# Issuing the second chunk of the first projection's weights from ScalarE instead of SyncE

## Chip, cores, metric

The kernel runs on one core of a Trainium2 chip. The metric is the device time of one execution in microseconds, the median over several runs.

## The reference

Two independent attention blocks, A and B, on their own inputs; the outputs are joined along the last axis. Per block, in bf16:

```python
# x: 16 x 32 x 1024, caches: 16 x 4 x 512 x 128, wq: 1024 x 4096, wo: 4096 x 1024
q = (x @ wq).reshape(B, Sq, Hq, Dh).transpose(0, 2, 1, 3)      # 32 heads of 128
k = repeat(k_cache, 8, axis=1); v = repeat(v_cache, 8, axis=1)
p = softmax(einsum("bhqd,bhkd->bhqk", q, k) * Dh ** -0.5)
out = einsum("bhqk,bhkd->bhqd", p, v).transpose(0, 2, 1, 3).reshape(B, Sq, Hq * Dh) @ wo
```

## The kernel before

All products of both blocks form one stream on PE (TensorE). Nothing can be multiplied before the first rows of A's `x` and `wq` have landed, so the first eight heads are projected chunk by chunk (a chunk is 128 of the 1024 input rows) while the loads come in. `TT` is 4 (tiles of 128 tokens), `NF` is 6 heads, `HC` is 4 chunks.

```python
load_x(0, TT // 2, TT, nc.scalar)        # x0b, 128 KB, on ACT
nc.scalar.preload_act_table_set("natural_log_exp_and_others")
load_x(0, 0, TT // 2)                    # x0a, 128 KB, on SP like all below
load_w0(0, 1, 0, NF // 2)                # w0a, 96 KB
load_w0(0, 1, NF // 2, NF)               # w0b, 96 KB
load_w0(1, 2, 0, NF)                     # w1, 192 KB
load_x(2, 0, TT)                         # x2, 256 KB
load_w0(2, 3, 0, NF)                     # w2, 192 KB
load_w0(3, 4, 0, NF)                     # w3, 192 KB
# ... on SP: the rest of w0, transposed x, wq, k, v

warm_up(22)                              # 22 products of constants, 128 columns
for k, ts in enumerate(((0, TT // 2), (TT // 2, TT))):
    transpose_x(0, *ts, nc.vector.tensor_copy)          # needs x0a, then x0b
    transpose_x(1, *ts, nc.scalar.copy, spare[k])
for ts in ((0, TT // 2), (TT // 2, TT)):
    first_heads(range(0, NF // 2), (0,), *ts)           # 6 products, need w0a
first_heads(range(NF // 2, NF), (0,))                   # 3 products, need w0b
first_heads(range(0, NF - 2), (1,))                     # 4 products, need w1
transpose_x(2, 0, TT, nc.vector.tensor_copy)            # need x2
transpose_x(3, 0, TT, nc.scalar.copy)
first_heads(range(NF - 2, NF), (1,))                    # 2 products, need w1
first_heads(range(NF), (2, 3))                          # need w2, w3
# ... everything else follows on PE in program order
```

Of the kernel before, what the change touches and what calls it, by code (L numbers as in the profile page):

```python
# [181 lines left out]
def kernel(  # L182
# [14 lines left out]
    nc = tc.nc  # L197
# [20 lines left out]
    def fast_path(ok_i):  # L218
        with ExitStack() as fctx:
# [235 lines left out]
            NF = REP - 2  # L455
# [8 lines left out]
            def load_x(d0, t0, t1, eng=nc.sync):  # L464
                eng.dma_start(
                    out=x_sb[:, t0:t1, d0 * P:(d0 + 2) * P],
                    in_=x_v[:, t0:t1, d0 * P:(d0 + 2) * P],
                )
# [4 lines left out]
                    in_=A_x.flatten_outer_dims()[:, d0 * P:(d0 + 2) * P],  # L473
                )

            def load_w0(d0, d1, h0, h1):
                nc.sync.dma_start(
                    out=w0[d0 // HC][:, d0 % HC:(d1 - 1) % HC + 1, h0 * DH:h1 * DH],
                    in_=wq_v[:, d0:d1, h0 * DH:h1 * DH],
                )  # L480

            load_x(0, TT // 2, TT, nc.scalar)
            nc.scalar.preload_act_table_set("natural_log_exp_and_others")
            load_x(0, 0, TT // 2)
            load_w0(0, 1, 0, NF // 2)
            load_w0(0, 1, NF // 2, NF)
            load_w0(1, 2, 0, NF)
            load_x(2, 0, TT)
            load_w0(2, 3, 0, NF)
            load_w0(3, 4, 0, NF)  # L490
# [184 lines left out]
    ok_i = flag.tile([1, 1], I32, name="ok_i")  # L675
    total = 2 * 2 * NG * QW
    ok = fast_path(ok_i)
    with tc.If(ok < total, preferred_fallthrough_block=True, label="general"):
        general_path(tc, problems, out_flat)
# [30 lines left out]
```

## Time and profile before

| kernel before | value |
|---|---|
| time, median of 3 runs | 343.63 us (343.56 to 343.73) |
| profiled execution | 343.01 us, span 341.2 us |
| PE busy | 98% of the span |
| first transpose, first product with weights | 3.28 us, 4.17 us |
| PE's step from half to full clock, by the distance of its starts | between 5.0 and 5.2 us |

A line of the timeline gives start, duration, engine, source line, operation, operands and count, then the idle time before and what ended it. PE is the array, PEld its weight loads, which run ahead of it: a wait of PEld is a wait of PE only if PE runs out of products. In the DMA view q1 is SP's queue and q10 is ACT's.

### The profile page before, as it was taken

What the parts mean: (1) busy time and instruction counts of PE and PEld (TensorE: products, weight loads), DVE (VectorE), ACT (ScalarE), POOL (GpSimd) and SP (SyncE); (2) the same over time, 40 slices, a digit from 0 to 9 for tenths busy, and PEclk for the clock granted to TensorE, in tenths of its full rate; (3) what the DMA queues carried; (4) which work ended last, traced back from release to release, by engine and by line L of the source; (5) the groups of instructions that cost most, each with busy time, mean ns of one, the idle gap of its engine ahead of it and who ended that gap; (6) DMA issues with size and microseconds to landing.
All of it is one profiled execution on the core that took longest, in us unless ns stands there. A gap on an engine that the chain in (4) does not pass through costs nothing.

```text
span 341.2 us, 5454 instructions
## 1 busy us (share of the span) xinstructions
PE 335.2 (98%) x2082; PEld 213.6 (63%) x2121; DVE 265.5 (78%) x336; ACT 185.9 (54%) x209; POOL 46.7 (14%) x206
## 2 busy tenths in 40 slices
PE   8999999999999999999999999999999999999996
PEld 6455666666666666666666666666666666666555
DVE  1046988888988898888888988879888888889540
ACT  3058666666667667666645545555555555555110
POOL 0001110011111111110012221222122101111100
PEclk9999999999999999999999999999999999999999
DMA  7999999999996987899999955998449997430001
GB/s 211 287 190 273 285 249 202 233 242 268 291 248 154 232 242 219 210 314 299 308 306 258 250 125 144 334 268 242 118 103 296 356 187 176 104 97 16 18 18 33
DMA packets 128094, 71.70 MB, mean 210 GB/s; under 512 B 75840, under 2 KB 127296, under 8 KB 128064
## 3 DMA queue, kind: packets, MB, share of 16 engines
q1 hardware_dynamic: 127264, 70.07, 84.1%
q0 software_dynamic: 384, 1.05, 0.9%
q8 instruction: 17, 0.28, 0.3%
q10 hardware_dynamic: 416, 0.20, 0.2%
q14 instruction: 13, 0.11, 0.1%
HBM read 50.86 MB, written 2.10 MB: 155 GB/s over the span
## 4 chain that ended last, share of the span: by engine, by line
PE 98%; issue 1%; ACT 0%; ACTq 0%
PE f_ps L320 32%; PE q_ps L301 28%; PE ob L425 17%; PE s_ps L357 16%; PE q_ps L534 4%; PE q_ps L516 1%; PE xT_ps L524 0%; ACT o_sb L329 0%; ACTq L329 0%
## 5 line engine op out<-in xcount | busy, mean ns | idle before, releaser
L365 ACT ACTIVATE p_sb<-s_ps,shift 128x1024 bf16<-128x1024 f32 x128 | 142.7, 1115 | 97.5 <-PE s_ps L357 88.1
L376 DVE TRANSPOSE_TENSOR_REDUCE parts<-p_sb 128x32 f32<-128x1024 bf16 x128 | 158.7, 1240 | 21.0 <-ACT p_sb L365 19.3
L320 PE MATMUL f_ps<-wo_sb,oT 128*128 128x512 bf16 (+1 forms) x525 | 128.2, 366 | 0.6
L301 PE MATMUL q_ps<-xT,wq_sb 128*128 128x512 bf16 x430 | 113.2, 379 | 0.5
L425 PE MATMUL ob<-p_sb,v_sb 128*128 128x256 bf16 x512 | 76.8, 273 | 0.8
L357 PE MATMUL s_ps<-qT,kT 128*128 128x256 bf16 x512 | 76.8, 273 | 0.0
L320 PEld LDWEIGHTS <-oT 128*128 128x128 bf16 x544 | 53.2, 98 | 35.3
L357 PEld LDWEIGHTS <-kT 128*128 128x128 bf16 x512 | 56.9, 113 | 28.3
L301 PEld LDWEIGHTS <-wq_sb 128*128 128x128 bf16 x448 | 43.8, 98 | 32.2
L425 PEld LDWEIGHTS <-v_sb 128*128 128x128 bf16 x512 | 50.1, 98 | 20.0
L447 DVE TENSOR_TENSOR oT<-r,ob 128x512 bf16<-128x512 f32 x64 | 43.9, 686 | 19.9 <-PE ob L425 19.4
L411 DVE STREAM_TRANSPOSE r<-rall 128x512 f32<-128x512 f32 x64 | 44.2, 691 | 1.1
L309 ACT CAST qT<-q_ps 128x512 bf16<-128x512 f32 x56 | 32.7, 583 | 16.5 <-PE q_ps L301 16.5
L394 POOL COPY half<-cs 64x32 f32<-64x32 f32 x32 | 6.5, 204 | 231.8 <-DVE cs L384 231.8
L329 ACT CAST o_sb<-f_ps 128x512 bf16<-128x512 f32 (+1 forms) x17 | 9.5, 559 | 23.6 <-PE f_ps L320 23.6
L534 PE MATMUL q_ps<-xT,w_sb 128*128 128x512 bf16 (+1 forms) x65 | 14.4, 379 | 0.1
L384 DVE TENSOR_REDUCE cs<-parts 128x32 f32<-128x128 f32 x32 | 12.1, 377 | 1.1
L406 DVE RECIPROCAL rall<-sums 128x32 f32<-128x32 f32 x32 | 10.2, 319 | 3.3 <-POOL sums L403 3.3
L534 PEld LDWEIGHTS <-w_sb 128*128 128x128 bf16 x67 | 6.8, 102 | 7.0 <-DMA w_sb<-in_A_wq_dram 0.2
L560 DVE CAST qT<-q_ps 128x512 bf16<-128x512 f32 x4 | 2.5, 684 | 10.2 <-PE q_ps L534 10.2
L331 POOL DMA_DIRECT2D out_dram<-o_sb x8 | 4.6, 574 | 29.3 <-ACT o_sb L329 29.3
L395 POOL TENSOR_TENSOR half<-half,cs 64x32 f32<-64x32 f32 x32 | 7.8, 243 | 2.6
(25 smaller groups left out, 44.7 us busy)
## 6 DMA issues: line engine op xcount, KB each, us to landing
v_sb<-in_A_v_cache_dram SPq DMA_DIRECT2D x16, 512.0 KB, 5.7
wq_sb<-in_B_wq_dram SPq DMA_DIRECT2D x8, 1024.0 KB, 5.7
wo_sb<-in_A_wo_dram SPq DMA_DIRECT2D x8, 1024.0 KB, 7.4
v_sb<-in_B_v_cache_dram SPq DMA_DIRECT2D x16, 512.0 KB, 4.7
wo_sb<-in_B_wo_dram SPq DMA_DIRECT2D x8, 1024.0 KB, 8.1
wq_sb<-in_A_wq_dram SPq DMA_DIRECT2D x5, 1024.0 KB, 5.8
wq_sb<-in_A_wq_dram SPq DMA_DIRECT2D x2, 512.0 KB, 6.7
kT<-in_A_k_cache_dram SPq DMA_TRANSPOSE x64, 4.4
```

Of the source, the lines that this page charges most:

```text
L301: nc.tensor.matmul(ps[:], lhsT=w[:, dc, (h % 4) * DH:(h % 4 + 1) * DH], rhs=xT[pr][:, dc, :], start=(dc == 0), stop=(dc == DC - 1),)
L309: nc.scalar.copy(out=qT[pr, g][:, :, hl, :], in_=ps[:].rearrange("p (b s) -> p b s", s=SQ),)
L320: nc.tensor.matmul(ps[:, 0:width], lhsT=oT[pr, tt][:, h, :], rhs=wo_tiles[pr, nh, h // REP][:, h % REP, off:off + width], start=(h == 0), ...
L357: nc.tensor.matmul(s_ps[:, c, :], lhsT=kT[:, i % GRP, c, :], rhs=qT[pr, g][:, b, :, :].rearrange("p h s -> p (h s)"), start=True, stop=True,)
L365: nc.scalar.activation(out=p_sb[:], in_=s_ps[:], func=ACTF.Exp, bias=shift[:], scale=SCALE)
L376: nc.vector.tensor_reduce(out=parts[k][:, q, :, :].rearrange("p c h -> p (c h)"), in_=st[i]["p"][:].rearrange("p c (h s) -> p (c h) s", s=SQ),
L384: nc.vector.tensor_reduce(out=cs[:], in_=parts.pop(k)[:].rearrange("p q c h -> p q h c"), axis=AX.X, op=ALU.add,)
L406: nc.vector.reciprocal(out=rall[:, k, :], in_=quad.pop(k)[:])
L411: nc.vector.transpose(out=r[:].rearrange("p n s -> p (n s)"), in_=rall[:, k, o * 2 * REP:(o + 1) * 2 * REP] .unsqueeze(2).to_broadcast([P, ...
L425: nc.tensor.matmul(ob[j][:, q, :], lhsT=v_sb[:, i % GRP, c, :], rhs=st[i]["p"][:, c, :], start=(c == 0), stop=(c == KC - 1),)
L447: nc.vector.tensor_tensor(out=out, in0=rcp.pop(j)[:].rearrange("p (q h) s -> p q h s", h=REP), in1=ob.pop(j)[:].rearrange("p q (h s) -> p ...
L534: nc.tensor.matmul(first_q[h][:, ts], lhsT=w0[dc // HC][:, dc % HC, h * DH:(h + 1) * DH], rhs=xT[0][:, dc, ts], start=(dc == 0 and t0 == 0 ...
```

## The change

The intent: w1 goes onto the second hardware queue, so that two queues feed the first products and SP is free 0.47 us earlier for what follows.

```diff
-            def load_w0(d0, d1, h0, h1):
-                nc.sync.dma_start(
+            def load_w0(d0, d1, h0, h1, eng=nc.sync):
+                eng.dma_start(
...
             load_w0(0, 1, NF // 2, NF)
-            load_w0(1, 2, 0, NF)
+            load_w0(1, 2, 0, NF, nc.scalar)
             load_x(2, 0, TT)
```

## The prediction

> **What bounds the kernel now.** I read four views: the page (busy table, chain of work that ended last), the same chain for the first 30 us, the timeline of the first 8 us engine by engine, and the DMA view in narrow windows, which gives each early load its own time from issue to landing. Names used below: x0a and x0b are the two halves (128 KB each) of the first part of x, w0a and w0b the two halves (96 KB each) of the first weight chunk, w1 the second chunk (192 KB, the load that moves), x2 the next part of x (256 KB), w2 the third chunk.
>
> From the page, PE and the clock first, then the chain:
>
> ```profile
> PE 335.2 (98%) x2082; PEld 213.6 (63%) x2121; DVE 265.5 (78%) x336; ACT 185.9 (54%) x209; POOL 46.7 (14%) x206
> ...
> PE 98%; issue 1%; ACT 0%; ACTq 0%
> ```
>
> PE is busy for 98% of 341.2 us and the chain is PE from start to end. A busy PE is not a PE at its peak, so I looked at starts: from 5.2 us on, 512-column products start 0.216 us apart, and the only longer step outside missing records is one of 0.239 us at 7.45. So there is no idle time downstream in which a delay of PE could disappear, nor one from which a gain could come: a shift of the first products moves the end by as much. The first products, in the chain:
>
> ```profile
> 0.73 0.19 issue
> 0.93 2.52 PE q_ps L516 x22
> 3.45 0.92 PE xT_ps L524 x8
> 4.37 2.58 PE q_ps L534 x13
> 6.95 0.45 PE xT_ps L524 x8
> 7.40 0.05 issue
> 7.45 10.76 PE q_ps L534 x49
> ```
>
> The reader is to see that the chain has no DMA in it: 22 warm-up products, 8 transposes, 13 products, 8 transposes, 49 products, with 0.05 us of issue between. The weight loads of PE show how close each transfer comes (start, duration, group):
>
> ```profile
> 3.27 0.83 PEld L524 LDWEIGHTS <-x_sb 128*128 128x128 bf16 x8
> 4.06 1.53 PEld L534 LDWEIGHTS <-w_sb 128*128 128x128 bf16 x9
> 5.79 0.67 PEld L534 LDWEIGHTS <-w_sb 128*128 128x128 bf16 x4 [0.20 <-DMA w_sb<-in_A_wq_dram]
> 6.59 0.63 PEld L524 LDWEIGHTS <-x_sb 128*128 128x128 bf16 x8
> ```
>
> The nine of the second row are six on w0a, then three on w0b; the third row is four on w1, the fourth the transposes of x2. Issue times and landings, from the SP timeline and three narrow DMA windows (KB, median us to landing):
>
> ```profile
> 1.26 1.39 SPq L477 DMA_DIRECT2D w_sb<-in_A_wq_dram  x3
> 2.69 0.43 SPq L465 DMA_DIRECT2D x_sb<-in_A_x_dram  x1
> ```
> ```profile
> w_sb<-in_A_wq_dram SPq DMA_DIRECT2D x1, 96.0 KB, 2.7
> ```
> ```profile
> w_sb<-in_A_wq_dram SPq DMA_DIRECT2D x1, 96.0 KB, 3.3
> ```
> ```profile
> w_sb<-in_A_wq_dram SPq DMA_DIRECT2D x1, 192.0 KB, 3.5
> ```
>
> The three issues of 1.39 us start at about 1.26, 1.75 and 2.21, so w0a lands at about 3.95, w0b at 5.05 and w1 at 5.75; x2 (3.9 us after 2.69) lands at about 6.55. PE takes them up at 4.06, 5.17, 5.79 and 6.59. The weight load of w1 does wait 0.20 us for its DMA, but that is PEld, which runs ahead of PE: the product before it starts at 5.71 and one lasts 0.216, so the next could not start before 5.93, and 5.93 is when it starts. The wait which the change wants to remove costs PE nothing. The slack is thin everywhere, though: 0.11 us for w0a and w0b, about 0.04 for w1 and x2.
>
> **What the Trainium skill says.** (1) "DMA: Bandwidth & Descriptors", section "Issuing engines are not separate DMA queues": DMAs from all engines run on the same 16 DMA engines, and issuing from several "will only save the time on the sequencer". The trace has 0.43 to 0.46 us per issue, so that is what is saved on SP. (2) "Perfetto Trace Analysis", section "DVE / Act Engine Instruction (TENSOR_ADD, Activation, etc)": the sequencer is free for the next instruction once one is pushed to the wait queue. The trace agrees on a compute instruction: ACT's register load of the flag starts at 331.3 and takes 0.47, beside a cast that runs from 331.23 for 0.59. It shows nothing of that kind for a table load. (3) Same page, section "DMA Instruction — HWDGE (DVE, Sync)": the descriptor generator is one block, shared and locked by the two sequencers. In the trace x0a (SP, 0.74) and x0b (ACT, 0.82) are issued 0.08 us apart without a longer issue time, but their data do not start together:
>
> ```profile
> q1 hardware_dynamic: 124, 0.06, 42.9%
> ```
> ```profile
> q10 hardware_dynamic: 197, 0.09, 71.7%
> q1 hardware_dynamic: 85, 0.06, 41.3%
> ```
>
> The first is the window 1.7 to 2.2 (q1 is SP's queue, q10 ACT's): half a microsecond with SP's packets alone; the second is 2.66 to 3.1, where ACT's dominate. So transfers of two queues start in order of issue, one behind the other, which fits a shared generator. (4) "TensorE: Matmul & The Clock Gate", part 1: the array runs at half clock until it has been busy for a free-running window of about 3.4 us. The trace agrees: products of 128 columns in the warm-up start 0.107 apart, transposes of the same width after 6.8 only 0.056; the step falls between 5.0 and 5.2.
>
> **The change part by part.** Program order on PE, DVE and POOL is the same. SP loses one issue of 0.43 us plus a gap of 0.04, so x2, w2 and all that follow are issued 0.47 us earlier until the queue is held up (the first DMA transpose already needs 1.52 us of SP). Worth on the path: zero, because PE waits for none of them. ACT gains one issue of 0.46 us after the table load of 1.28 us; its next work is a copy at 3.92, so that is free. What matters is the new place of w1 in the order of transfers. If ACT's sequencer passes the table load, w1 is issued at 1.31 to 1.78, between w0a (1.26) and w0b (1.75), instead of behind w0b. Served in that order, 192 KB stand ahead of or beside the 96 KB of w0b. Both together were in by 5.75 before, and the bytes up to there are the same, so w0b lands between its old 5.05 and 5.75; I take the middle, 5.4 (an estimate). PE needs it at 5.17 and takes up a landing within 0.04 (5.79 against 5.75): its weight load comes at 5.44, 0.27 us late, and the product with it. w1 is then there, and x2 (same bytes ahead of it) lands by 6.55, while PE now wants it at 6.59 + 0.27. Sum: 0 (SP) + 0 (ACT) + 0.27 (w0b) - 0 (w1) = +0.27 us, 343.63 + 0.27 = 343.9, +0.08%.
>
> **The rivals.**
> A. Nothing moves, or a trace of gain (25%). For it: between 3.2 and 4.6 us the DMA engines move only about 150 GB/s, where 350 are seen soon after, so w1 may fill a hole and w0b stay at 5.05. Even then nothing is won: all that PE loses to early data (its starts in the trace, less the usual step) is 0.035 us before the first transpose, 0.085 before the fifth, 0.024 at 7.45, and the change speeds up neither x0a nor x0b. 343.5 to 343.65.
> B. ACT's sequencer is held by the table load (20%), so w1 is issued at 2.6 to 3.05, behind x2 (now at 2.21). Against it: reading (2) above; for it: no run so far has a DMA behind a table load. w1 would then land between 5.75 and x2's old 6.55, say 6.2 (an estimate), where PE needs it by 5.79: about +0.45, 344.1.
> C. w0a is hit too (within my main case or 5% by itself): w1 shares the engines with it from 2.9 us and its slack is 0.11. A stall at 4.06 lies in the half-clock window; if that window then counts as not busy enough, full clock comes one window of 3.4 us later, which costs half of it, 1.7 us: 345.3. Against it: a stall of 0.2 leaves that window over 90% busy.
> D. Gain downstream from transfers that come 0.47 us earlier: against it stand the PE starts without gaps; worth zero.
>
> **The range and the chances.** Weights: main case 50% at +0.27, A 25% at -0.05, B 20% at +0.45, C 5% at +1.7: 0.135 - 0.01 + 0.09 + 0.085 = +0.3, so 343.9. The three times of before lie within 0.17 us, so noise is smaller than the effect; low 343.4 (rival A and noise), high 344.7 (B with a late landing). 2% is 6.9 us, more than 4 times the worst rival: within 2% 0.99, faster 0.003, slower 0.007.
>
> **What would show it.** In the changed kernel: (a) ACT's second DMA issue starts at about 1.3 if the sequencer passes the table load, at 2.6 if not; (b) q10 has 128 packets more, and they lie before or among those of w0b; (c) w0b's time to landing is about 3.65 us instead of 3.3, and its weight load is at 5.3 to 5.7 instead of 5.17, with a wait for the DMA; (d) the wait of 0.20 for w1 is gone; (e) the chain of PE from 7.45 on is the same, shifted by the delay; (f) the step to full clock stays at about 5.1. I am wrong if the 49 products begin before 7.4 (a real gain that I see no source for), if w0b keeps its 5.05, or if the end shifts by another amount than the first products do.

## The result and the profile after

| | before | after |
|---|---|---|
| median of 6 runs each | 343.60 us (343.02 to 343.73) | 343.52 us (342.68 to 343.77) |
| profiled execution | 343.01 us | 342.68 us |

A ratio is the mean time of one kernel's runs over the mean of the other's of the same rounds, so not quite the ratio of the medians. Here it is 0.9997, with a 95% interval of 0.9984 to 1.001: the same. But the profiled pair differs by 0.33 us, and the traces show where. First the chain of the kernel after, for its first 30 us:

```profile
4.41 2.23 PE q_ps L534 x13
6.63 0.45 PE xT_ps L524 x8
7.08 11.68 PE q_ps L534 x54
```

The products behind the second transposes begin at 7.08 (6.63 + 0.45); before, those transposes ended at 7.40, 0.32 us later. Two things moved. One is the weight loads of the kernel after:

```profile
3.37 0.77 PEld L524 LDWEIGHTS <-x_sb 128*128 128x128 bf16 x8 [0.19 <-DMA x_sb<-in_A_x_dram]
4.12 2.02 PEld L534 LDWEIGHTS <-w_sb 128*128 128x128 bf16 x13
6.26 0.65 PEld L524 LDWEIGHTS <-x_sb 128*128 128x128 bf16 x8
```

All 13 of chunk 0 and 1 are one row now: no wait on w0b and none on w1. The first transpose waits for x0a a little longer than before (3.37 against 3.27). The other is the clock. The six products of 256 columns on w0a, kernel before and kernel after, from the groups by form in the first 9 us (busy us, mean ns of one):

```profile
L534 PE MATMUL q_ps<-xT,w_sb 128*128 128x256 bf16 x6 | 1.3, 376 | 0.0
```
```profile
L534 PE MATMUL q_ps<-xT,w_sb 128*128 128x256 bf16 x6 | 0.9, 288 | 0.0
```

Such a product takes 418 to 421 ns at half clock and 273 at full clock, so 288 says that five of the six ran at full clock; 376 says that most did not. The starts put the step at 4.4 us after against 5.1 before. Nothing in the change aims at that, and the kernel before alone has the step at 5.1, 4.6 and 3.75 us in its three profiles (table below). PE's "granted clock" is 1.00 in both, because the record behind it begins only at the step. A step 0.73 us earlier (4.37 against 5.10) is worth half of that, 0.36 us (an estimate: at half clock a product takes twice as long), which is about all that the pair differs by. What the kernel before would have done with so early a clock, this pair cannot tell; the experiments had to.

The ACT timeline of the kernel after, and the loads issued between 1.71 and 2.2 us (or still at it) with their time to landing:

```profile
0.82 0.46 ACTq L465 DMA_DIRECT2D x_sb<-in_A_x_dram  x1
1.31 1.28 ACT L483 ACT_TABLE_LOAD   x1 [1.31 <-PEq L694]
1.34 0.45 ACTq L477 DMA_DIRECT2D w_sb<-in_A_wq_dram  x1
```
```profile
w_sb<-in_A_wq_dram ACTq DMA_DIRECT2D x1, 192.0 KB, 3.3
w_sb<-in_A_wq_dram SPq DMA_DIRECT2D x1, 96.0 KB, 3.2
```

The sequencer passes the table load: w1 is issued at 1.34, beside it. w1 lands at 1.34 + 3.3 = 4.6 (5.75 before), w0b at 1.75 + 3.2 = 4.9 (5.03 before). What happened to w0b is in the window 3.2 to 3.85, kernel before and kernel after:

```profile
DMA packets 140, 0.09 MB, mean 144 GB/s; under 512 B 18, under 2 KB 140, under 8 KB 140
...
q1 hardware_dynamic: 139, 0.09, 54.2%
```
```profile
DMA packets 246, 0.25 MB, mean 377 GB/s; under 512 B 24, under 2 KB 246, under 8 KB 246
...
q10 hardware_dynamic: 113, 0.16, 64.1%
q1 hardware_dynamic: 133, 0.09, 41.8%
```

SP's queue carries as much as before (0.09 MB), and w1 comes on top of it on ACT's queue (0.16 MB).

### The profile page after: what moved, and what is told of

The parts are those of the page before. It is cut to its first block, busy times and chain, and to the rows that moved or that the text cites. A ratio compares the mean times of both kernels' runs of the same rounds, so it can differ in the third digit from the quotient of the medians.

```text
span 340.9 us, 5493 instructions
## 1 busy us (share of the span) xinstructions
PE 336.9 (99%) x2121; PEld 213.2 (63%) x2121; DVE 265.6 (78%) x336; ACT 185.8 (54%) x209; POOL 46.7 (14%) x206
## 4 chain that ended last, share of the span: by engine, by line
PE 99%; ACT 0%; issue 0%; ACTq 0%
PE f_ps L320 32%; PE q_ps L301 28%; PE ob L425 16%; PE s_ps L357 16%; PE q_ps L534 4%; PE q_ps L516 1%; PE xT_ps L524 0%; ACT o_sb L329 0%; ACTq L329 0%
## 5 line engine op out<-in xcount | busy, mean ns | idle before, releaser
L320 PE MATMUL f_ps<-wo_sb,oT 128*128 128x512 bf16 (+1 forms) x544 | 132.4, 367 | 0.0
L301 PE MATMUL q_ps<-xT,wq_sb 128*128 128x512 bf16 x448 | 117.0, 379 | 0.0
```

What stands on the lines that cost most here:

```text
L301: nc.tensor.matmul(ps[:], lhsT=w[:, dc, (h % 4) * DH:(h % 4 + 1) * DH], rhs=xT[pr][:, dc, :], start=(dc == 0), stop=(dc == DC - 1),)
L320: nc.tensor.matmul(ps[:, 0:width], lhsT=oT[pr, tt][:, h, :], rhs=wo_tiles[pr, nh, h // REP][:, h % REP, off:off + width], start=(h == 0), ...
```

## The experiments

Twelve runs were made, all with right results, in three calls, each on another chip (7, 4 and 2), so times are compared within a call; the runs of the kernel before of one call are shared. All edits are to the lines shown above. For each profile I worked out from the starts in the trace where PE stepped to full clock (by interpolation in the product whose distance changes), and how long it stood between products beyond the step of the clock at that time ("stall"; the wait for x0a before the first transpose is not in it). The table at the end has all of them.

### Changed kernel and kernel before once more

Edits: none.

> The changed kernel once more. In its first profile PE reaches the 54 products at 7.08 us against 7.40 before, but the step of PE to full clock also came earlier, at 4.2 to 4.5 us against 5.0 to 5.3. Theory 1 (clock): the 0.3 us in the traces come from the moment of the step to full clock, which changes from run to run; the change itself is worth under 0.1 us. Then the medians of this and of before differ by under 0.2 us, and in a profile with a late step (5 us) this kernel too reaches the 54 products at about 7.4. Theory 2 (two queues): the early data is worth 0.3 us; then the products come at about 7.1 also with a late step, and the median is 0.3 us under that of before.

> The kernel before once more, as control. Theory 1: the step to full clock lies elsewhere in this profile, and the products from 7.40 move by half of that shift; if it comes at 4.3, PE asks for w0b, w1 and x2 before they land (5.03, 5.75, 6.55 in the first profile) and has to wait, so at least part of the 0.3 us is not won. Theory 2: products stay at about 7.4 whatever the clock. Time 343.6 +- 0.2, ratio 1.000.

Measured: changed kernel 343.27 us, ratio 1.0004 (0.999 to 1.0018); kernel before as its own control 343.25 us, ratio 0.9996 (0.9983 to 1.001). The two profiles happen to have the same clock (step at 4.6 us), so they are the comparison that the first pair was not. Weight loads of the kernel before, second profile, then of the changed kernel, second profile:

```profile
3.99 0.90 PEld L534 LDWEIGHTS <-w_sb 128*128 128x128 bf16 x6
5.40 1.19 PEld L534 LDWEIGHTS <-w_sb 128*128 128x128 bf16 x7 [0.51 <-DMA w_sb<-in_A_wq_dram]
...
7.32 1.69 PEld L534 LDWEIGHTS <-w_sb 128*128 128x128 bf16 x9
```
```profile
3.38 0.77 PEld L524 LDWEIGHTS <-x_sb 128*128 128x128 bf16 x8 [0.20 <-DMA x_sb<-in_A_x_dram]
4.14 2.10 PEld L534 LDWEIGHTS <-w_sb 128*128 128x128 bf16 x13
6.36 0.65 PEld L524 LDWEIGHTS <-x_sb 128*128 128x128 bf16 x8
6.97 2.12 PEld L534 LDWEIGHTS <-w_sb 128*128 128x128 bf16 x11
```

With an early step PE finishes its six products on w0a at 5.0 and the kernel before has no w0b until 5.36: PE itself stands for 0.40 us. The changed kernel has it at 4.94 and does not stand. Against that its first transpose starts 0.14 later; together it is 0.35 us ahead at the weight load after x2 (6.97 against 7.32). So each theory got a part: the products of before did not move up with the clock, because PE had to wait, as theory 1 had allowed for. The stall that the second queue removes is there only with an early clock; theory 2 had the gain in any case. And the runs without profile do not show 0.35 us.

### Same order of data, one queue

```diff
             load_w0(0, 1, 0, NF // 2)
+            load_w0(1, 2, 0, NF)
             load_w0(0, 1, NF // 2, NF)
-            load_w0(1, 2, 0, NF)
```

> w1 between w0a and w0b, all on SP: the order in which the changed kernel's data moved, without the second queue. If the order alone does it, w1 lands at about 4.6 to 4.9 and w0b within 0.3 us of that. If the second queue adds something, w0b (now issued at 2.2 instead of 1.75) lands 0.4 us or more later than 4.90 and PE waits for it 0.3 to 0.5 us before the fourth product group. Theory 1: time within 0.3 us of before. Theory of the prediction (w0b behind w1 costs): +0.2 to +0.5 us.

Measured: 343.84 us, ratio 1.0016 (1.0001 to 1.0031), which is 0.55 us; the interval, 0.03 to 1.06 us, does not decide between the theories. The weight loads that need w0b:

```profile
5.77 1.19 PEld L534 LDWEIGHTS <-w_sb 128*128 128x128 bf16 x7 [0.64 <-DMA w_sb<-in_A_wq_dram]
```

w1 landed at 5.44 and w0b at 5.73, and PE stood for about 0.4 us before w0b's products. This is what the prediction had feared for the changed kernel, and it does happen when the same order runs on one queue: w0a, w1 and w0b are all in by 5.73 here (5.65 to 5.83 in the three profiles of the kernel before), by 4.90, 4.94 and 5.06 in the three of the changed kernel. So the order alone does not bring the data earlier; with the second queue it came 0.6 to 0.9 us earlier. That queue also lets w1 and w0b be issued 0.41 and 0.47 us earlier, and this pair of runs does not separate the two.

### A late w1 on purpose

```diff
-            load_w0(1, 2, 0, NF)
             load_x(2, 0, TT)
             load_w0(2, 3, 0, NF)
+            load_w0(1, 2, 0, NF)
```

> w1 behind x2 and w2 on SP: a late w1 on purpose. w1 then lands at about 7.0 (where w2 landed before), PE wants it at 5.8 and stands for 1.2 us. If the front of PE sets the end one to one, the time is 1.2 us longer (344.8); if idle time downstream absorbs it, it stays at 343.6.

Measured: 344.60 us, ratio 1.0036 (1.002 to 1.0051), which is 1.2 us on 343.3. The weight loads on w1, then the first after x2:

```profile
7.17 0.55 PEld L534 LDWEIGHTS <-w_sb 128*128 128x128 bf16 x4 [1.36 <-DMA w_sb<-in_A_wq_dram]
8.44 0.61 PEld L534 LDWEIGHTS <-w_sb 128*128 128x128 bf16 x4
```

The weight load after x2 is at 8.44 against 7.18, 1.26 later, and PE's last product starts at 339.13 against 337.87, 1.26 later. The front sets the end one to one.

### No warm-up

```diff
-            warm_up(22)
+            warm_up(0)
```

> The kernel before without its 22 warm-up products (right result, PE idle until 3.2 us). Full clock should then come at about 6.7 us or later[...] instead of 4.3 to 5.1, so PE asks for each load later. If the gain of the second queue depends on an early step to full clock, PE of this kernel has no stall on w0b and w1, and the products after x2 start about 1 us later than in the kernel before; time 0.8 to 1.3 us longer (344.2 to 344.6).

> The changed kernel without its warm-up products, to be set against the run above. If the second queue's gain of 0.33 us in the traces is a stall on w0b that only an early clock shows, then here the two are alike: products after x2 within 0.1 us of the run above, or 0.1 later because x0a lands 0.1 later beside the second issue. If the second queue speeds PE in any phase, this kernel is 0.3 us ahead.

Measured: without warm-up the kernel before takes 344.70 us, ratio 1.0032 (1.0014 to 1.0049), 1.1 us longer (344.2 to 344.6 was expected); the changed kernel 344.41 us, 1.0025 (1.0009 to 1.0041). In the first PE ran at half clock until 8.7 us (the six products take 421 ns each) and did not stand for w0b or w1.

That is the half of the claim that it settles: with a late clock, one queue is fast enough. The comparison with the changed kernel is spoilt: the two reach the weight load after x2 at 8.76 and 8.78 us, alike as expected, but for reasons that cancel: the changed kernel stood for w0a, which landed only at 4.67 us instead of 4.08 to 4.21 (w1's packets ran beside it, but no more of them than with warm-up, 0.15 MB between 3.2 and 3.85 against 0.14 to 0.17, so the cause is open), and its clock then stepped up at 7.8, 0.9 us earlier than the other's. Its weight loads on w0a and w0b:

```profile
4.71 1.41 PEld L534 LDWEIGHTS <-w_sb 128*128 128x128 bf16 x8 [0.90 <-DMA w_sb<-in_A_wq_dram]
```

### One queue, one issue less

```diff
-            load_w0(0, 1, 0, NF // 2)
-            load_w0(0, 1, NF // 2, NF)
+            load_w0(0, 1, 0, NF)
```

> One queue, but w0a and w0b as one load of 192 KB, so that SP issues w1 and x2 0.47 us earlier, as in the changed kernel, without the second queue. If the hole between 3.2 and 3.85 us (128 to 168 GB/s on one queue, 367 to 377 with two) is bound by the rate of issue, the hole is smaller (over 250 GB/s), and w1 lands at about 5.1, x2 at 6.0. If it belongs to what one queue moves at that time (slow packets), it stays at 130 to 170 and w1 lands at 5.6 or later. PE waits for w0 in one piece until about 4.4 either way.

Measured: 344.00 us in 2 runs, ratio 1.0014 (0.9996 to 1.0032). The hole between 3.2 and 3.85 was gone (294 GB/s), which speaks for the rate of issue, but w1 still landed at 5.70, because 217 and 227 GB/s followed from 3.85 to 5.5. Both theories got half. The edit also doubles the bytes of a row: 142 packets carried 0.19 MB in that window, where 140 carried 0.09 in the kernel before. So larger pieces are a rival to the rate of issue, and no run separates them; the cause of the hole stays open.

### w0b on ACT, w1 on SP

```diff
-            load_w0(0, 1, NF // 2, NF)
-            load_w0(1, 2, 0, NF, nc.scalar)
+            load_w0(0, 1, NF // 2, NF, nc.scalar)
+            load_w0(1, 2, 0, NF)
```

> Two queues with the loads in the order of need: w0b on ACT behind its part of x, w1 on SP. If issue order sets the order of data, w0b lands at about 4.3 to 4.6 and w1 at about 4.9 (PE asks for them at 4.9 and 5.4), so PE has no stall even with the earliest clock and the front is like the changed kernel's or up to 0.05 us ahead. Time within 0.3 us of before; in the trace the products after x2 at 6.8 to 7.0 if the clock steps before 4.7.

Measured: 343.44 us, ratio 0.9991 (0.9978 to 1.0005). w0b landed at 4.20, before the expected 4.3 to 4.6, but w1 on SP only at 6.21, later than in any profile of the kernel before: from 3.85 to 4.6 the engines moved 122 GB/s. PE did not stand, because its clock stepped late (6.0 us). With an early clock it would have waited for w1 by some 0.6 us, an estimate from when PE began its first product on w1 in the first two profiles of the changed kernel (5.61 and 5.71) and this landing (6.21); no run shows that. Two queues alone do not fill the hole; which load sits on which matters.

### The changed kernel and the kernel before a third time, and two more orders

```diff
 # e10, against the changed kernel: w0b and w1 both on ACT
-            load_w0(0, 1, NF // 2, NF)
+            load_w0(0, 1, NF // 2, NF, nc.scalar)
 # e11, against the changed kernel: x0a in two halves on two queues
+            load_x(0, 1, TT // 2, nc.scalar)
             load_x(0, TT // 2, TT, nc.scalar)
 ...
-            load_x(0, 0, TT // 2)
+            load_x(0, 0, 1)
 ...
-            warm_up(22)
+            warm_up(19)
```

> The changed kernel a third time, now with a model of the front: from the first transpose to the product after x2, PE needs 3.06 us at full clock; the rest of that stretch is half of the time at half clock plus stalls. So far stalls were 0.01 and 0.03 us in the two profiles of this kernel, 0.09 and 0.42 in the two of before, and the step to full clock came anywhere from 4.3 to 6.9 us. Expected: stalls under 0.1 us whatever the step, w0b landed by 5.1, w1 by 4.9. Time: if an early clock is the rule in unprofiled runs too, 0.3 us under before (0.999); if late steps are as common, within 0.1 us (1.000).

> The kernel before a third time, control for the three above and a third look at its stalls. Expected: w0b at 5.0 to 5.4, w1 at 5.7 to 5.9; a stall on w0b of about (w0b landing - 4.9) if the clock steps before 4.7, none if it steps after 5.1. Ratio 1.000.

> w0b and w1 both on ACT, x2 and the rest on SP. If what fills the hole is that SP's queue carries less, both land by 4.9 and x2 by 6.0, stalls are nil and the front equals the changed kernel's at the same clock. If ACT's queue shows the same hole when it carries three loads in a row, w1 lands at 5.5 or later and PE with an early clock (it asks at 5.4) waits for it. Time within 0.3 us of before.

> The one term left in front of PE is x0a, which lands at 3.06 to 3.34 us. Here x0a is halved: one 64 KB piece on SP, one on ACT, then x0b on ACT, w1 behind it, and 19 warm-up products instead of 22 (they end at 2.92). If landing follows bytes, both pieces land at about 2.9 and the first transpose starts 0.3 us earlier; at half clock that is worth 0.15 to 0.3 us at the end. If the fixed part of a load rules (x0a needs 2.5 us of which 1.0 us is data), the third issue on ACT delays x0b and w1 by 0.45 us, PE stands before the fifth transpose, and nothing is won.

Measured: changed kernel 343.55 us, ratio 1.0011 (0.9996 to 1.0026); kernel before as control 343.24 us, 0.9997 (0.9984 to 1.0011); w0b and w1 on ACT 344.09 us, 1.0026 (1.0012 to 1.004); x0 in three 344.00 us, 1.0025 (1.0004 to 1.0046).

The changed kernel missed its expectation (stalls under 0.1 us), and here is one place where the gain can go. Third profile of the changed kernel, then of the kernel before:

```profile
4.25 2.06 PEld L534 LDWEIGHTS <-w_sb 128*128 128x128 bf16 x13
6.90 0.45 PEld L524 LDWEIGHTS <-x_sb 128*128 128x128 bf16 x8 [0.58 <-DMA x_sb<-in_A_x_dram]
```
```profile
4.92 0.33 PEld L534 LDWEIGHTS <-w_sb 128*128 128x128 bf16 x3 [0.34 <-DMA w_sb<-in_A_wq_dram]
5.69 0.55 PEld L534 LDWEIGHTS <-w_sb 128*128 128x128 bf16 x4 [0.44 <-DMA w_sb<-in_A_wq_dram]
6.50 0.51 PEld L524 LDWEIGHTS <-x_sb 128*128 128x128 bf16 x8 [0.26 <-DMA x_sb<-in_A_x_dram]
...
7.87 1.19 PEld L534 LDWEIGHTS <-w_sb 128*128 128x128 bf16 x7 [0.76 <-DMA w_sb<-in_A_wq_dram]
```

w0b and w1 are in time in the changed kernel, but now x2 came late (6.85 instead of 5.99 and 6.13) and PE stood 0.25 us. The kernel before with a very early clock (3.75 us) stood for w0a, w0b and w1 and then 0.42 us for w2. A slow stretch now comes later. Totals of the window 5.5 to 7.0, first profiles of the kernel before and the kernel after:

```profile
DMA packets 510, 0.49 MB, mean 324 GB/s; under 512 B 39, under 2 KB 510, under 8 KB 510
```
```profile
DMA packets 322, 0.35 MB, mean 230 GB/s; under 512 B 27, under 2 KB 322, under 8 KB 322
```

The three profiles of the kernel before have 324, 312 and 304 GB/s here, the three of the changed kernel 230, 250 and 239. That it is the earlier hole, moved, is not shown: in the first profiles SP's packets took 54% of the engines' time in the hole and 102% in this window. By the third chunk the lead is thin (w2: 7.06, 7.18, 7.83 before; 6.97, 7.17, 7.37 after), by w3 none is left (7.77, 7.79, 8.38 before; 8.19, 7.77, 7.92 after).

The two other orders lost, by about 0.9 us, where within 0.3 us had been hoped for. With three early issues on ACT, x0a landed at 3.58 and the first transpose started 0.35 us late; w1, third on ACT's queue, came at 5.93. x0 in three pieces gave the first transpose its 0.3 us (2.92), but x0b, now the second issue on ACT, landed at 4.06 and PE stood 0.76 us for it.

### All profiles

Times in us; "front" is the start of the first weight load after x2's transposes, "last" that of PE's last product.

| kernel, profile | full clock from | stalls of PE | front | last | last - front |
|---|---|---|---|---|---|
| before, first | 5.1 | 0.09 (x0b) | 7.181 | 337.867 | 330.686 |
| before, second | 4.6 | 0.40 (w0b) | 7.316 | 338.003 | 330.687 |
| before, third | 3.75 | 0.1 (w0a), 0.23 (w0b), 0.11 (w1), then 0.42 (w2) | 6.960 | 338.069 | 331.109 |
| after, first | 4.4 | 0.01 | 6.863 | 337.552 | 330.689 |
| after, second | 4.6 | 0.02 | 6.968 | 337.655 | 330.687 |
| after, third | 4.75 | 0.09 (w0a), 0.25 (x2) | 7.303 | 337.990 | 330.687 |
| w1 second, one queue | 5.3 | 0.4 (w0b) | 7.687 | 338.373 | 330.686 |
| w1 behind w2 | 5.6 | 1.03 (w1) | 8.439 | 339.126 | 330.687 |
| w0b on ACT | 6.0 | 0 | 7.610 | 338.297 | 330.687 |
| w0b and w1 on ACT | 6.2 | 0.06 (x0b); first transpose 0.38 late | 7.898 | 338.585 | 330.687 |
| x0 in three | 7.2 | 0.76 (x0b) | 8.400 | 339.087 | 330.687 |
| w0 in one | 7.0 | 0.40 (w0) | 8.289 | 338.976 | 330.687 |
| before, no warm-up | 8.7 | 0.07 (x0b) | 8.763 | 339.429 | 330.666 |
| after, no warm-up | 7.8 | 0.84 (w0a) | 8.781 | 339.469 | 330.688 |

The packed trace has a record of the granted clock too. In 12 of the 14 profiles it begins at the step, within 0.05 us of this table; w0b on ACT and w0b and w1 on ACT have none. The stretch at full clock lasts 337.92 us in eight profiles and 334.51 in the four with a step at 7.0 or later: two lengths only, 3.41 us apart.

The last column is the most useful result. From the end of the front to the last product 330.69 us pass, in 12 of 14 profiles to within 3 ns; the largest exception is the one that stood for w2. After the last product the span goes on for 3.35 us, but for 3.42 in w0 in one and 3.77 in x0 in three. Apart from these, the difference between the kernels is made in the first 9 us.

## Why the prediction was right or wrong

- The 2% and the range held: 343.52 us lies in 343.4 to 344.7. Of the two later medians of the changed kernel 343.55 lies in it and 343.27 is 0.13 below. The expected 343.9 missed by 0.4: the time lies in the lowest tenth of the range, which was there for rival A and noise, so for the main case the range held by luck. The reason given holds: the end follows the front one to one.
- Its sum did not. The step that failed is w0b's landing at 5.4, late by 0.27 us: it landed at 4.90, 4.94 and 5.06. The order of data was as predicted (w1's packets beside and ahead of w0b's), and so was the passing of the table load, so rival B is out. What was missed is that the engines had room: 144 GB/s in the window where they then moved 377. The prediction had seen that hole and put it into rival A, at 25%, instead of into the main case. Where the order alone is tried, on one queue, the predicted stall comes (about 0.4 us). The 0.27 was moreover counted on PEld (5.44 - 5.17). PE's first product on w0b started at 5.28, so even a landing at 5.4 would have cost PE only 0.17. Of its own signs of being wrong one came true, products that begin before 7.4 (7.08), and the step to full clock did not stay at 5.1; by the estimate above the early clock explains both.
- Rival A was right that w0b is not hurt, and wrong that nothing can be won. "The wait which the change wants to remove costs PE nothing" was read from one profile, whose clock stepped at 5.1. When the clock steps at 4.6, the same kernel stands 0.40 us for w0b. The slack of 0.11 us was a slack at one phase of the clock.
- Rival C (w0a hit, full clock late) showed itself in part: w0a landed at 4.08, 4.10 and 4.21 instead of 3.79 to 3.92, which cost 0 to 0.09 us, and 0.84 us in the run without warm-up. Full clock came late (6.2 to 7.2) in all three warmed-up kernels that stood 0.38 us or more before 4.6, but at 6.0 in one that never stood; the link is not shown.
- The expected mean, +0.3, came from the wrong term. The changed kernel's 17 runs have a mean of 343.46 us, the 45 runs of the kernel before 343.39, with standard errors of 0.10 and 0.05. That is +0.07 with an uncertainty of about 0.2: no gain and no loss that these runs can see. The traces say what it can be made of: w0b and w1 come in time (up to -0.4 with an early clock, nothing with a late one), x0a and w0a land about 0.1 to 0.4 us later (up to +0.2, an estimate from the waits for them), and a slow stretch falls on x2 in one of three profiles (+0.25). How often each happens in runs without a profile stays open.
- Each timed run has its mean granted clock, to three decimals. In the changed kernel 12 of 17 runs have 1.000 (mean 343.26 us) and 5 have 0.999 (343.95); in the kernel before, of the 39 runs with this figure, 30 have 1.000 (343.23) and 9 have 0.999 (343.84). Within each group the two kernels differ by no more than the noise (0.02 and 0.11 us, standard errors about 0.1). So most of the scatter goes with the clock and not with the change. All six profiles of these two kernels are of 1.000 runs; what happens in the others, no trace shows. In the three profiles of other kernels that read 0.999 or 0.998 the step came at 7.0 to 7.8 us.

None of the variants beat both kernels: w0b on ACT has the lowest ratio, 0.9991, but its interval reaches 1.0005.

## What to carry to other kernels

A transfer moved to a second queue can arrive much earlier (here w1 by 1.1 us) and still be worth nothing, if the engine that waits for it was not going to be idle, or if the next transfers pay for it. Before changing the order of early loads, find the fixed distance from the front to the end, since then one number of a trace, the end of the front, tells what a change did to that one execution, here mostly to within nanoseconds, while the times of one kernel scatter by up to 1.6 us (342.68 to 344.29). And take several profiles: slack at a start depends on a clock whose step lies elsewhere in each run.

## What the Trainium skill lacked or had wrong

- "TensorE: Matmul & The Clock Gate", part 1, puts the step to full clock at about 4 us of sustained work, within 0.5 us. With the same 22 warm-up products it came between 3.75 and 6.0 us in the kernels that had not stood for 0.38 us or more before it, which is 2.8 to 5.1 us after the first of these products (0.93). The page's advice not to fit to a fixed count agrees. It does not say that a profile's mean granted clock can read 1.00 over a start at half clock, as it did here, where the record begins at the step.
- "DMA: Bandwidth & Descriptors", section "Issuing engines are not separate DMA queues", has a second issuing engine save only sequencer time, which is 0.47 us here. In the same order of data the three loads landed by 4.90 to 5.06 us with two queues and by 5.73 with one, 0.7 to 0.8 earlier, and between 3.2 and 3.85 us two queues moved 331 to 377 GB/s where one moved 168. With w0b in place of w1 on the second queue they were in only by 6.21. Over the first 8 us the page is right: w3 lands no earlier.
- No page that I found says of a table load on ACT whether it holds back a DMA issue behind it; there is only the rule for engine instructions in general that the prediction cites. It does not: the issue starts at 1.34 us beside a load that runs from 1.31 to 2.60.
- No page that I found gives the size of what follows from more early issues on ACT: x0a, issued on SP at 0.74 in all kernels, landed at 3.05 to 3.25 us with one issue on ACT before 2.3 us and the warm-up, at 3.13 to 3.34 with two, at 3.58 with three of full size. The cause is open.
